# Query features of two groups in one set of products, and three calls of a hand-written schedule moved

## Chip, core and metric

The kernel runs on one core of a Trainium2 chip. The metric is the device time of one launch in microseconds (us). The median of three runs of the kernel before is 263.09 us (263.04 to 263.23). One more execution was taken with the hardware profiler: it took 262.89 us, and its trace spans 261.1 us. Clock times below ("at 62.89") are microseconds from the start of that trace.

The engines are TensorE (PE in the profile; its weight loads are PEld), VectorE (DVE), ScalarE (ACT), GpSimd (POOL) and SyncE (SP), which here only starts DMAs. Each works through its own list of instructions in order and waits on semaphores for the others.

## What is computed

An attention with polynomial features, followed by two dense layers with ELU between them. Batch, heads, rows and head size are 4, 4, 1088 and 32; `r` is 8; the dense layers are 128 to 2048 to 128.

```python
def phi(x):                                   # 64 features of a row
    a, b = x @ S1.T, x @ S2.T                 # 8 and 8
    return (a[..., :, None] * b[..., None, :]).reshape(..., 64)
q_p, k_p = phi(q), phi(k)
kv  = einsum('bhsf,bhsd->bhfd', k_p, v)       # per batch and head, 64 x 32
z   = k_p.sum(axis=2)                         # per batch and head, 64
num = einsum('bhsf,bhfd->bhsd', q_p, kv)
den = einsum('bhsf,bhf->bhs', q_p, z) + 1e-6
x   = (num / den), heads side by side         # 4352 rows of 128
h   = x @ w_in                                # 4352 x 2048
out = where(h > 0, h, exp(min(h, 0)) - 1) @ w_out
```

The denominator is computed without the 64 features: it is the sum over eight places of b times "b against z", and the program divides the factors by it (`an`) before it forms the 64 products.

## The kernel before

**Groups.** The 4352 rows make nine groups of 512 (the last has 256). Group `g` covers 16 tiles' worth of one batch: groups 2 and 3 are batch 1, tiles of 64 columns 0 to 7 and 8 to 15 of its transposed queries `qT[1]`.

**Steps.** The dense layers are done in 64 steps `(g, cp)`, where `cp` is one of eight pairs of 128 hidden columns. The list `steps` (L954) fixes their order: groups 0 and 1 alternate up to step 15, then groups 2, 3, ... follow with eight steps each. The loop at L1051 issues one step: `mm1` (first layer, PE, into two PSUM banks "h"), then whatever the schedule hangs on this step with `at`, then the ELU of the first half (`elu`: two ACT passes L811 and L813, one DVE pass L819 that writes `gg`), then the calls hung on with `mid`, the ELU of the second half, the calls of `late`, and last the second layer of the step before the previous one. That second layer is `mm2` or `mm2_blocks` for groups 0 and 1; from step 16 on it is `mm2_seven` (L720), which makes 7 block products out of 8 from sums that POOL forms: `sums7` (three POOL instructions per step, tile `tt`, L701 to L704) and `weights7` (L684, sums of the weights in `SS`, four POOL instructions per call).

**The attention is spread over these steps** by the table of `at`, `mid` and `late` calls (L970 to L1048). All engines are in order, so the place in this table is the place in each engine's queue. The parts that matter here:

- Keys of a batch: `transp` (DVE, 1088 columns) turns the keys; `KF_late` makes features on PE; `KO` the 64 products; `KA` (L425, PE) sums them against v; `sums_out` (L984) copies z on ACT (`ZC`), turns kv on DVE (`KT_out`, L436) and sends it through DRAM with five DMAs on SP; `turn` (`Z`, PE) and `turned` (`Z_out`, DVE, then `Z_share`, two POOL instructions) put z into the weights `SWs`.
- Queries of a group: `queries` (L658) takes the two "h" banks of the next step and two more banks, and issues into all four: the output products `q5` of one group (half f=0), the features `q1` (L533) of another, and `q5` again (f=1). `q1` is 16 products on 32x32 pieces of the array, one for each piece. `q1_out` (L544) is four DVE transposes out of the four banks into `abw`. Then on DVE come `q2_den` (L558: product, sum, reciprocal, product: the division), `q2_half` (L623, 64 products) and `q4` (L631, a transpose into `qpT`); `q5` and the ACT copies `q5_out` give the group's `xg`, the input of `mm1`. `q2_a` (L617) is an ACT copy of the divided factors into PSUM.

A "h" bank has four buffers, two per step, so the PE part of step n that writes the banks of step n+1 must wait for the DVE pass L819 of step n-1. The next `mm1` in turn must wait for the transposes that read them.

For batch 1 and the groups 2 and 3, the schedule before says:

```python
for b, (n_t, n_f, n_o, n_a, n_z) in enumerate(
        ((4, 6, (7, 9), 11, 12), (12, 16, (17, 18), 19, 20), (15, 16, (23, 24), 27, 28)), 1):
for n, g, nx in ((13, None, 2), (15, 2, 3), (22, 3, 4), (30, 4, 6), (46, 6, 8), (62, 8, None)):
    at(n, queries, g, nx, n + 1)
```

that is: sums of batch 1 in step 11, z in step 12, features of group 2 in step 13, output of group 2 with features of group 3 in step 15, output of group 3 with features of group 4 in step 22.

Of the kernel before, what the change touches and what calls it, by code (L numbers as in the profile page):

```python
# [12 lines left out]
F32 = mybir.dt.float32  # L13
# [9 lines left out]
def _ap(ap: bass.AP, free):  # L23
    return dataclasses.replace(ap, ap=[list(ap.ap[0])] + [list(x) for x in free])
# [3 lines left out]
def kernel(  # L28
# [21 lines left out]
    nc = tc.nc  # L50
    B, H, S, D = q.shape
    R = S1.shape[0]
    P = 128
# [3 lines left out]
    NP = NC // 2  # L57
# [7 lines left out]
    work = ctx.enter_context(tc.tile_pool(name="wk", bufs=2))  # L65
# [7 lines left out]
    qT = [const.tile([FD, NT, 64], F32, name=f"qT{b}") for b in range(2)] * 2  # L73
    qE = const.tile([FD, 2, 64], F32, name="qE")
# [69 lines left out]
    for x, (eng, src) in enumerate(((nc.sync, S1), (nc.scalar, S2))):  # L144
        rs = slice(R * x, R * x + R)
# [150 lines left out]
    SWs = const.tile([FD, B, 4, R], F32, name="SWs")  # L296
# [180 lines left out]
    NQ = (NH + 7) // 8  # L477
    qn = [min(8, NH - 8 * g) // 2 for g in range(NQ)]
    abw, ans, qp, qpT, xg, xps = {}, {}, {}, {}, {}, {}
# [48 lines left out]
    def quarter_of(g, w):  # L528

        n = un[g] // 2  # L530
        return (*half_tile(g + n * w // 8, n * w % 8), n)

    def q1(g, ps, o, opened):  # L533
        for w in range(4):
            b, t, n = quarter_of(g, w)
            qs = qE[:, b:b + 1, :] if g == NQ - 1 and b < 2 else qT[b][:, t:t + n, :]
            for r in range(4):
                rows = slice(32 * r, 32 * r + 32)
                nc.tensor.matmul(ps[r][32 * w:32 * w + 32, o:o + 64 * n], SWs[rows, b].rearrange("p x r -> p (x r)"),  # L539
                                 qs[rows].rearrange("p t s -> p (t s)"),  # L540
                                 start=not opened, stop=True, skip_group_check=True, tile_position=(32 * r, 32 * w))
        abw[g] = ps, o

    def q1_out(g):  # L544
        (ps, o), n = abw[g], un[g]
        pair = n > 4
        abw[g] = work.tile([P, H * n if pair else H * 4, 4 * R], F32, name="abw", tag="abwp" if pair else "abw",
                           bufs=1 if pair else 2)
        m = H * n // len(ps)
        for r in range(len(ps)):  # L550
            nc.vector.transpose(abw[g][:, m * r:m * r + m, :].rearrange("p m y -> p (m y)"),
                                ps[r][:, o:o + 32 * m])
# [105 lines left out]
    def queries(g5, g1, n):  # L658

        hs[steps[n]] = [psum.tile([P, 512], F32, name="h", tag="h", bufs=4) for c in range(2)]  # L660
        ps = hs[steps[n]] + [psum.tile([P, 512], F32, name="qps", tag="aux") for _ in range(2)]
        if g5 is not None:
            q5(g5, ps, 0)
        if g1 is not None:
            q1(g1, ps, 256 if g5 is not None else 0, g5 is not None)
        if g5 is not None:
            q5(g5, ps, 1)
# [293 lines left out]
    def at(n, f, *a):  # L961
        extra.setdefault(n, []).append((f, *a))

    def mid(n, f, *a):
        extra.setdefault((n, 0), []).append((f, *a))

    def late(n, f, *a):
        extra.setdefault((n, 1), []).append((f, *a))
# [25 lines left out]


    for b, (n_t, n_f, n_o, n_a, n_z) in enumerate(
            ((4, 6, (7, 9), 11, 12), (12, 16, (17, 18), 19, 20), (15, 16, (23, 24), 27, 28)), 1):
        (late if b == 2 else at)(n_t, transp, kT, "k", b, 0, NT)
        at(n_f, KF_late, b, n_f + 1 if b == 3 else None)
        (mid if b == 3 else late)(n_f, KF_late_out, b)  # L1000
        for half in range(2):
            if b == 1 and half == 0:
                at(n_o[half], KO, b, half, nc.gpsimd)
            else:
                late(n_o[half] - 1, KO_a, b, half)
                at(n_o[half], KO_b, b, half)
        at(n_a, KA, b)
        late(n_a, sums_out, b)
        at(n_z, turn, b)
        at(n_z, turned, b)  # L1010
# [1 line left out]
    at(19, transp, qT, "q", 2, 0, NT)  # L1012
    late(24, transp, qT, "q", 3, 0, NT)

    for n, g, nx in ((13, None, 2), (15, 2, 3), (22, 3, 4), (30, 4, 6), (46, 6, 8), (62, 8, None)):
        at(n, queries, g, nx, n + 1)
        if g is not None:
            mid(n, q5_out, g)
        if nx is not None:
            mid(n, q1_out, nx)  # L1020
        if g is not None and len(units[g]) > 1:
            late(n, q5_out, g, 1)
    late(13, q2_den, 2)
    late(13, q2_half, 2, 0)
    mid(14, q4, 2)
    late(19, q2_den, 3)
    late(19, q2_a, 3, 0)
    late(19, q2_half, 3, 0)
    late(20, q4, 3)
# [13 lines left out]
    late(59, q2_half, 8, 0)  # L1043
    late(60, q4, 8)

    late(12, weights7, slice(NP - 2, NP))
    late(13, weights7, slice(0, 3))
    late(15, weights7, slice(3, NP - 2))  # L1048

    N = len(steps)  # L1050
    for n in range(2, N):  # L1051
        g, cp = steps[n]
# [29 lines left out]
        g, cp = before  # L1082
# [10 lines left out]
    g = NQ - 2  # L1093
# [53 lines left out]
```

## Time and profile before

| | us |
|---|---|
| median of three runs | 263.09 |
| profiled execution | 262.89 |
| its span | 261.1 |
| PE busy in the span | 255.5 (98%) |
| DVE, ACT, POOL busy | 188.1, 183.2, 158.9 |
| step 14 (first layer, `mm2`, nothing else on PE) | 65.08 to 68.51 |
| step 18 (first layer, `mm2_seven`, nothing else on PE) | 81.26 to 84.50 |

The page of the profile gives the busy time of each engine, the chain of work that ended last, and groups of instructions. Its timeline lists each engine's instructions in order: start, time from the first start to the last end, line, operation, output and inputs, count, and in brackets how long the engine was idle before and what released it. One product of the program in fp32 can be recorded as two instructions, so the 16 products of `q1` appear as 32. The ends of matmuls are modelled; their starts are not, so lengths on PE are taken here from one start to the next. The granted PE clock is 9 tenths or more in all 40 slices of the span.

### The profile page before, as it was taken

What the parts mean: (1) busy time and instruction counts of PE and PEld (TensorE: products, weight loads), DVE (VectorE), ACT (ScalarE), POOL (GpSimd) and SP (SyncE); (2) the same over time, 40 slices, a digit from 0 to 9 for tenths busy, and PEclk for the clock granted to TensorE, in tenths of its full rate; (3) what the DMA queues carried; (4) which work ended last, traced back from release to release, by engine and by line L of the source; (5) the groups of instructions that cost most, each with busy time, mean ns of one, the idle gap of its engine ahead of it and who ended that gap; (6) DMA issues with size and microseconds to landing.
All of it is one profiled execution on the core that took longest, in us unless ns stands there. A gap on an engine that the chain in (4) does not pass through costs nothing.

```text
span 261.1 us, 9678 instructions
## 1 busy us (share of the span) xinstructions
PE 255.5 (98%) x4107; PEld 158.6 (61%) x4107; DVE 188.1 (72%) x356; ACT 183.2 (70%) x358; POOL 158.9 (61%) x202
## 2 busy tenths in 40 slices
PE   8899999999999999999999999999999999999994
PEld 7652333354346657666666666665666666668994
DVE  6899999999978987997477575744455446674641
ACT  2469878767568387775687777775877777777792
POOL 4420007006276978788678798888588888887410
PEclk9999999999999999999999999999999999999999
DMA  6998089022011111012100200020001100110021
GB/s 175 331 358 216 3 246 261 7 72 53 4 29 19 28 25 26 3 15 31 28 3 1 30 13 3 0 33 13 3 0 24 21 4 0 21 24 3 3 35 28
DMA packets 28506, 14.29 MB, mean 55 GB/s; under 512 B 21392, under 2 KB 26640, under 8 KB 28464
## 3 DMA queue, kind: packets, MB, share of 16 engines
q1 hardware_dynamic: 28032, 13.32, 20.7%
q8 instruction: 32, 0.52, 0.8%
q10 hardware_dynamic: 368, 0.30, 0.3%
q14 instruction: 10, 0.08, 0.1%
q0 software_dynamic: 64, 0.07, 0.1%
HBM read 11.31 MB, written 2.36 MB: 52 GB/s over the span
## 4 chain that ended last, share of the span: by engine, by line
PE 97%; DVE 1%; ACT 0%; issue 0%; DVEq 0%
PE h L256 45%; PE pb L740 17%; PE pa L740 13%; PE o L256 5%; PE pb L716 4%; PE ol L256 3%; PE idle L264 1%; PE h L645 1%; PE kv L430 1%; PE qps L645 1%; PE abp L340 1%; PE h L539 1%; PE qtp L598 1%; DVE qp L586 1%; PE xps L605 0%; PE kfps L362 0%
## 5 line engine op out<-in xcount | busy, mean ns | idle before, releaser
L256 PE MATMUL h<-xg,W 128*32 128x512 f32 (+3 forms) x880 | 130.6, 538 | 0.4 <-ACT xg L611 0.4
L819 DVE SCALAR_TENSOR_TENSOR gg<-e,h 128x512 f32<-128x512 f32 x128 | 85.7, 681 | 51.7 <-ACT e L813 48.3
L811 ACT ACTIVATE e<-h 128x512 f32<-128x512 f32 x128 | 75.5, 590 | 42.9 <-PE h L256 42.8
L813 ACT ACTIVATE e<-e 128x512 f32<-128x512 f32 x128 | 80.9, 632 | 3.8
L701 POOL TENSOR_TENSOR tt<-gg 128x512 f32<-128x512 f32 x50 | 64.2, 1285 | 30.0 <-DVE gg L819 24.9
L256 PEld LDWEIGHTS h<-xg,W 128*32 128x32 f32 (+1 forms) x880 | 42.5, 123 | 43.3 <-issue 34.9
L704 POOL TENSOR_TENSOR tt<-gg,tt 128x256 f32<-128x256 f32 x50 | 36.9, 738 | 3.9
L703 POOL TENSOR_TENSOR tt<-tt,gg 128x256 f32<-128x256 f32 x50 | 36.8, 735 | 3.9
L740 PEld LDWEIGHTS pa<-gg,W 128*64 128x64 f32 (+1 forms) x472 | 23.8, 128 | 24.0 <-issue 23.3
L740 PE MATMUL pa<-gg,W 128*64 128x128 f32 (+1 forms) x472 | 30.4, 274 | 0.0
L740 PE MATMUL pb<-tt,SS 128*64 128x128 f32 (+1 forms) x456 | 29.4, 273 | 0.0
L740 PEld LDWEIGHTS pb<-tt,SS 128*64 128x64 f32 (+1 forms) x456 | 22.6, 128 | 0.0
L740 PE MATMUL pa<-tt,SS 128*64 128x128 f32 (+1 forms) x276 | 20.9, 273 | 0.0
L740 PE MATMUL pb<-tt,W 128*64 128x128 f32 (+1 forms) x244 | 19.7, 273 | 0.0
L740 PE MATMUL pb<-gg,SS 128*64 128x128 f32 (+1 forms) x244 | 19.7, 273 | 0.0
L134 POOL TENSOR_TENSOR raw<-raw,tiny 128x512 f32<-128x512 f32 x1 | 1.0, 1044 | 24.7 <-DVE raw L129 24.7
L256 PE MATMUL o<-gg,W 128*32 128x512 f32 x128 | 15.3, 595 | 0.0
L740 PEld LDWEIGHTS pa<-tt,SS 128*64 128x64 f32 (+1 forms) x276 | 13.5, 125 | 0.0
L740 PEld LDWEIGHTS pb<-gg,SS 128*64 128x64 f32 (+1 forms) x244 | 12.6, 127 | 0.0
L740 PEld LDWEIGHTS pb<-tt,W 128*64 128x64 f32 (+1 forms) x244 | 12.6, 127 | 0.0
L716 PE MATMUL pb<-gg,W 128*32 128x256 f32 x192 | 11.6, 380 | 0.0
L871 DVE SCALAR_TENSOR_TENSOR gg<-e,h 128x256 f32<-128x256 f32 x16 | 6.6, 418 | 6.4 <-PE h L256 3.2
(156 smaller groups left out, 274.3 us busy)
## 6 DMA issues: line engine op xcount, KB each, us to landing
raw<-in_moe_w_in_dram SPq DMA_DIRECT2D x8, 256.0 KB, 6.2
raw<-in_moe_w_out_dram SPq DMA_DIRECT2D x8, 256.0 KB, 6.5
out_dram<-ob SPq DMA_DIRECT2D x112, 16.0 KB, 1.6
hd_k<-in_k_dram SPq DMA_DIRECT2D x3, 544.0 KB, 7.8
hd_q<-in_q_dram SPq DMA_DIRECT2D x3, 544.0 KB, 8.1
v<-in_v_dram SPq DMA_DIRECT2D x4, 288.0 KB, 7.0
v<-in_v_dram SPq DMA_DIRECT2D x4, 256.0 KB, 8.5
kvs<-kvd SPq DMA_DIRECT2D x13, 32.0 KB, 1.8
```

The costliest lines, as they stand in the source:

```text
L256: nc.tensor.matmul(dst[c:c + tile], lhs[:, c:c + tile], rhs, skip_group_check=True, tile_position=(0, c), **kw)
L264: nc.tensor.matmul(idle[c:c + tile, :cols], ones[:, :tile], ones[:, :cols], skip_group_check=True, tile_position=(0, c))
L645: nc.tensor.matmul(ps[w][32 * r:32 * r + 32, :64 * n], kvs[b][rows, r, f, :], qpT[g, i][rows, o:o + 2 * n, f, :], start=(f == 0), stop=(f ...
L701: nc.gpsimd.tensor_tensor(_ap(t[:, 0], [[4 * P, 2], [P, 2], [1, P]]), _ap(gs[g, cp][:, 0, P:], [[4 * P, 2]] + us), _ap(gs[g, cp][:, 0], [[ ...
L703: nc.gpsimd.tensor_tensor(t[:, 1], t[:, 2], b11, op=ADD)
L704: nc.gpsimd.tensor_tensor(t[:, 3], b21, t[:, 1], op=SUB)
L716: nc.tensor.matmul(acc[1][0][r:r + width[0], 256 * hi:256 * hi + 256], lhs[:, w:w + width[0]], gg[:, c, 256 * u:256 * u + 256], start=(cp ...
L740: nc.tensor.matmul(bank[r:r + width[0], P * col:P * col + P], lhs[:, w:w + width[0]], rhs[:, u], start=(first and i in ((0,) if g == 1 els ...
L811: nc.scalar.activation(e, hs[g, cp][c][:, :n], RELU, scale=-1.0)
L813: nc.scalar.activation(e, e, EXP, scale=-1.0)
L819: nc.vector.scalar_tensor_tensor(gs[g, cp][:, c, :n], es[g, cp][:, c, :n], -1.0, hs[g, cp][c][:, :n], op0=ADD, op1=MAX)
L871: nc.vector.scalar_tensor_tensor(gs["last", k // 2][:, k % 2, :2 * P], es["last", k // 2][:, k % 2, :2 * P], -1.0, hs["last", k][:, :2 * P ...
```

## The change

`q1` of group 2 now takes the same 128 columns of group 3 along: each of its 16 products streams 256 columns in two pieces, tile t and tile t+8. It is issued in step 12 instead of 13, and `q1` of group 3 is gone from step 15. Two of its four transposes come ahead of the ELU of step 12, two in the middle of it, each for both groups, into one tile `abw2`. To have z in time, batch 1's `KA` and `sums_out` go from step 11 to 10, `turn` and `turned` from 12 to 11. The turning of batch 2's keys goes from step 12 to 14. `q2_den` of group 2 goes from late in step 13 to late in step 12, its `q4` from the middle of step 14 to its beginning, and `q2_den` of group 3 from late in step 19 to the middle of step 15. Of POOL's `weights7`, the last two pairs stay in step 12 but earlier, pairs 0 to 2 go from step 13 to 15 and pairs 3 to 5 from 15 to 16.

```diff
     def q1(g, ps, o, opened):
         for w in range(4):
             b, t, n = quarter_of(g, w)
-            qs = qE[:, b:b + 1, :] if g == NQ - 1 and b < 2 else qT[b][:, t:t + n, :]
+            m, qs = 64 * n, qE[:, b:b + 1, :] if g == NQ - 1 and b < 2 else qT[b][:, t:t + n, :]
+            qs = qs.rearrange("p t s -> p (t s)")
+            if g == 2:
+                m, qs = 2 * m, _ap(qs, [[8 * 64, 2], [1, m]])
             for r in range(4):
                 rows = slice(32 * r, 32 * r + 32)
-                nc.tensor.matmul(ps[r][32 * w:32 * w + 32, o:o + 64 * n], SWs[rows, b].rearrange("p x r -> p (x r)"),
-                                 qs[rows].rearrange("p t s -> p (t s)"),
-                                 start=not opened, stop=True, skip_group_check=True, tile_position=(32 * r, 32 * w))
+                nc.tensor.matmul(ps[r][32 * w:32 * w + 32, o:o + m], SWs[rows, b].rearrange("p x r -> p (x r)"),
+                                 qs[rows], start=not opened, stop=True, skip_group_check=True,
+                                 tile_position=(32 * r, 32 * w))
         abw[g] = ps, o
+
+    def q1_out_two(rs):
+        if 3 not in abw:
+            abw[2, 3] = abw[2][0]
+            t = work.tile([P, 2, 4 * H, 4 * R], F32, name="abw2", tag="abw2", bufs=1)
+            abw[2], abw[3] = t[:, 0], t[:, 1]
+            abw[2, 0] = t
+        n = 4 * H // 4
+        for r in rs:
+            nc.vector.transpose(abw[2, 0][:, :, n * r:n * r + n, :].rearrange("p g m y -> p g (m y)"),
+                                abw[2, 3][r][:, :64 * n].rearrange("p (g m) -> p g m", g=2))
...
-            ((4, 6, (7, 9), 11, 12), (12, 16, (17, 18), 19, 20), (15, 16, (23, 24), 27, 28)), 1):
+            ((4, 6, (7, 9), 10, 11), (14, 16, (17, 18), 19, 20), (15, 16, (23, 24), 27, 28)), 1):
...
-    for n, g, nx in ((13, None, 2), (15, 2, 3), (22, 3, 4), (30, 4, 6), (46, 6, 8), (62, 8, None)):
+    for n, g, nx in ((12, None, 2), (15, 2, None), (22, 3, 4), (30, 4, 6), (46, 6, 8), (62, 8, None)):
         at(n, queries, g, nx, n + 1)
         if g is not None:
             mid(n, q5_out, g)
-        if nx is not None:
+        if nx == 2:
+            at(n, weights7, slice(NP - 2, NP))
+            at(n, q1_out_two, (0, 1))
+            mid(n, q1_out_two, (2, 3))
+        elif nx is not None:
             mid(n, q1_out, nx)
...
-    late(13, q2_den, 2)
+    late(12, q2_den, 2)
     late(13, q2_half, 2, 0)
-    mid(14, q4, 2)
-    late(19, q2_den, 3)
+    at(14, q4, 2)
+    mid(15, q2_den, 3)
     late(19, q2_a, 3, 0)
...
-    late(12, weights7, slice(NP - 2, NP))
-    late(13, weights7, slice(0, 3))
-    late(15, weights7, slice(3, NP - 2))
+    late(15, weights7, slice(0, 3))
+    late(16, weights7, slice(3, NP - 2))
```

## Prediction

> **What bounds the kernel now.** I read the busy times and the chain of waits on the page first.
>
> ```profile
> PE 255.5 (98%) x4107; PEld 158.6 (61%) x4107; DVE 188.1 (72%) x356; ACT 183.2 (70%) x358; POOL 158.9 (61%) x202
> ...
> PE 97%; DVE 1%; ACT 0%; issue 0%; DVEq 0%
> ```
>
> PE is both the busiest engine and 97% of the chain that ends last. So time is won only where PE gets less work, or where it loses time that its busy count hides. The waits of PE, for the whole span, name five, all in the start-up (2.0 us together); asked from 50 us on, the view is empty. But ends on PE are modelled, so a wait can hide inside a "busy" stretch. I therefore took PE's timeline and compared steps from start to start. A bare step with `mm2` is 3.43 (step 14, 65.08 to 68.51), one with `mm2_seven` 3.24 (step 18). What a step has over that is the price of its extras:
>
> ```profile
> 61.02 1.94 PE L256 MATMUL h<-xg,W 128*32 128x512 f32 x16
> 62.89 0.30 PE L539 MATMUL h<-qT,SWs 32*32 32x128 f32 x2
> ...
> 63.33 1.94 PE L716 MATMUL pb<-gg,W 128*32 128x256 f32 x32
> 65.08 1.91 PE L256 MATMUL h<-xg,W 128*32 128x512 f32 x16
> ...
> 68.51 1.91 PE L256 MATMUL h<-xg,W 128*32 128x512 f32 x16
> 70.35 0.30 PE L645 MATMUL h<-qpT,kvs 32*32 32x128 f32 x2
> ...
> 70.67 0.41 PE L539 MATMUL h<-qT,SWs 32*32 32x128 f32 x3
> ...
> 71.16 0.31 PE L645 MATMUL h<-qpT,kvs 32*32 32x128 f32 x2
> ...
> 71.76 1.93 PE L256 MATMUL o<-gg,W 128*32 128x512 f32 x16
> 73.50 1.90 PE L256 MATMUL h<-xg,W 128*32 128x512 f32 x16
> ```
>
> Step 13 takes 65.08 - 61.02 = 4.06, so `q1` of group 2 costs 4.06 - 3.43 = 0.63. Step 15 takes 73.50 - 68.51 = 4.99: its three stages (`q5`, `q1` of group 3, `q5`) cost 1.56, the middle one 71.16 - 70.67 = 0.49 of it.
>
> Step 22 has the same three stages, with 256 columns in `q1`:
>
> ```profile
> 95.47 1.94 PE L256 MATMUL h<-xg,W 128*32 128x512 f32 x16
> 97.34 0.67 PE L645 MATMUL h<-qpT,kvs 32*32 32x128 f32 x3
> 97.72 0.30 PE L645 MATMUL qps<-qpT,kvs 32*32 32x128 f32 x2
> ...
> 100.88 0.61 PE L256 MATMUL h<-xg,W 128*32 128x512 f32 x4
> ```
>
> It takes 5.41, 2.17 over 3.24. Per piece of the array, steps 15, 46 and 30 stream 384, 576 and 768 columns in such three stages, and cost 1.56, 1.88 (179.20 to 184.33) and 2.22 (125.07 to 130.53): a line of 0.66 / 384 = 1.72 ns a column. Step 22 with 512 should cost 1.78. It costs 0.39 more, and the gap from 97.34 to 97.72 is where: the second bank is not free. DVE, ACT and POOL tell why.
>
> ```profile
> 92.01 0.27 ACT L621 COPY qa<-an 128x128 f32<-128x128 f32 x1 [3.91 <-DVE an L573]
> ```
> ```profile
> 90.55 1.28 POOL L701 TENSOR_TENSOR tt<-gg 128x512 f32<-128x512 f32 x1
> ```
> ```profile
> 90.59 1.39 DVE L573 TENSOR_TENSOR an<-abw,den 128x128 f32<-128x128 f32 x1
> ...
> 96.41 1.25 DVE L819 SCALAR_TENSOR_TENSOR gg<-e,h 128x512 f32<-128x512 f32 x2
> ```
>
> `q2_den` of group 3, late in step 19, ends at 91.98. ACT's copy of `an` stands in front of the ELU of step 20, so ACT idles 3.91 us, and starts on a bank that PE finished some 2 us earlier. ACT works without a gap until 98.06 to catch up; the `gg` of step 21 end at 97.66, and at 97.72 PE goes on. L573 itself takes 1.39, where the same line took 0.29 at 66.39 with POOL idle; here it ends 0.15 after POOL's L701.
>
> **Part by part.**
>
> *One `q1` of 256 columns.* Removed: 0.63 (step 13), and the middle stage of step 15. What step 15 keeps is bounded twice: 1.56 - 0.49 = 1.07, and step 62, which has `q5` twice with 64 columns each and no `q1` (233.01 to 237.19, 4.18 - 3.24 = 0.94), plus 128 columns more, 0.22, = 1.16. I take 1.10, nearer to the same step's own row. Added in step 12: 0.63 + 128 x 1.72 ns = 0.85 (bounds: 0.10 more than now, the difference of the rows of 0.30 and 0.40 for one product of 128 and 256, and 0.63 more, two separate stages). Sum: 2.19 now, 1.95 then: **-0.24**; with the ends of 1.07 to 1.16 and 0.73 to 0.85, -0.18 to -0.39; with the outermost 1.26 even +0.2. That the columns come in two pieces should not matter: `q5` reads its columns in pieces too and lies on the same line.
>
> [...]
>
> *`KA` and `Z` one step earlier.* The same products, 1.18 and 0.07, in another step: 0 for PE if nothing is late. `KA` would start at 49.48 + 1.72 = 51.2; the last of its inputs, L389, ends at 50.10. ACT's copy of z follows its ELU of step 10 (ended at 53.0); `Z` comes on PE at 55.9. The kv transpose (0.24) now stands ahead of the turning of `qT[1]` (1.31), which ends near 56.4, and z comes behind it at 56.9 (it waits for `Z`, done by 56.2; behind it stand the `gg` of step 11); POOL's two (0.42) make `SWs` ready by 57.4. SP's DMAs of batch 1 are now issued earlier, though behind the same held load of the last queries, whose buffer frees with `qT[1]`, 0.2 later; before, the last was issued by 64.4 and such a one lands in 1.8; `q5` wants them at 70.5.
>
> *Step 12.* Steps 11, 12, 13 start on PE at 54.09, 57.59 and 61.87. `q1` starts near 59.4 and needs the `gg` of step 11, done near 58.3: 1.1 to spare. The tightest place is behind it: `mm1` of step 13 needs the first two transposes. DVE first rounds the last weights (57.86 to 60.37 now, 2.51; now waiting for ACT until 58.3), to 60.8. They wait for `q1` itself too, but it is through by 60.3; a later one would hold all of DVE's queue, the `gg` of step 12 first. A pair of 256-column transposes takes 0.78 (99.68), so they are read out at 61.2 and 61.6. Margin 0.6, and 1.1 for the second bank. Cost 0; each us beyond costs one.
>
> *Group 2 to step 15.* The division of group 2 ends at 64.7 (1.26 as now, POOL's sums over at 62.6), `gg` of step 13 at 66.0, products (1.15) and turn (1.17) at 68.3, `gg` of step 14 at 69.5; `q5` starts at 70.5. Margin 1.0, against 0.1 now (70.27 to 70.35). DVE is then behind by the two key turns (2.45, one of them new here) and the division of group 3 (1.26): the second `gg` of step 15 ends at 74.4, as it does now (74.48), and the output turn at 75.1. PE writes that bank at 76.3. No cost.
>
> *`weights7`.* 4 x 0.6 = 2.35 on POOL goes from idle time (62.87, step 13) to behind the sums of step 15 in place of the other block, which follows the sums of step 16. POOL's sums of step 17 so begin at 85.0 instead of 84.78 and end at 87.9. PE's `mm2_seven` of step 19 needs the last of them at its seventh product, 88.5: 0.6 to spare.
>
> *Division of group 3 off step 19.* DVE loses 2.5 there (89.50 to 91.98), ACT copies at 88.2, the `gg` of step 21 end near 96.2, and PE wants the bank at 97.1. **The hidden 0.39 goes.** Next late are those `gg` themselves, with 0.9 to spare. In its new place POOL is free but for a 0.23 copy, because POOL's next sums wait for the `gg` that stands behind the division.
>
> [...]
>
> After step 22 every step is 3.24 or 3.25 with no hidden gap, to the end, so what is won stays won.
>
> Sum: -0.24 - 0.39 = **-0.63**: 262.89 to 262.26 for a profiled execution. The median lies 0.20 above that execution, so 262.5.
>
> **Rivals.**
>
> 1. *Only the products count* (14%). The gap in step 22 stays, because ACT or POOL is late there for another reason: -0.24, 262.85. For it: ACT is nearly full from 92 to 98. Against: its 3.91 idle names `an`.
>
> 2. *PE waits for the transposes in step 13* (10%). If rounding or transposes end over 0.6 late, the excess is paid; a us late leaves -0.23, 262.85. Against: the four rounding rows are even (0.43 to 0.72).
>
> [...]
>
> 4. *The long product does not run as one.* If 256 columns in two pieces cost two stages, +0.2 instead of -0.24, with the gap gone -0.2: 262.9. Counted with the forecast's spread.
>
> **Chances.** Forecast 70%: its spread of -0.2 to -0.8 us (the ends of the first part with 0.39) is faster by over 0.2% (0.53 us, about what a measurement here can tell from no change) in 57 of the 70, within it in 13. Rival 1, 14, within. Rival 2: 8 within, 2 slower. Rival 3: 6 slower. Together 57, 35, 8. The range 262.2 to 263.1 takes in the forecast's ends, 262.3 to 262.9, with 0.1 for the spread of the runs (263.04 to 263.23), and rivals 1, 2 and 4; rival 3 lies outside.
>
> **What will show it.** Step 12 on PE about 0.85 over 3.43 and step 15 about 1.10 over; step 22 about 1.78 over 3.24, with no gap in its first `q5`; ACT's `qa` copy without its idle. Wrong if a step from 12 to 21 is longer than 3.43 or 3.24 plus its extras: in 13 through L551's successor, in 19 through `tt`.

## The result, and the profile after

The changed kernel takes 262.60 us (median of 19 runs, 262.30 to 263.15), the kernel before 263.08 (19 runs): a ratio of 0.9983, 95% interval 0.9976 to 0.9991. That is 0.48 us less; the forecast, 262.5, would have been 0.58 less than this median. Over three series (42 runs) the changed kernel's median is 262.62.

The first profiled execution after took 263.07 us, with a span of 261.1, as before. It is one of the long ones of its series, whose median span is 260.6. What made it long can be seen, and is taken up below. The page gives the same picture of the bound, with 32 matmul records fewer on PE (16 products in two records each):

```profile
PE 255.4 (98%) x4075; PEld 158.9 (61%) x4075; DVE 186.6 (71%) x352; ACT 183.3 (70%) x358; POOL 158.9 (61%) x202
...
PE 97%; DVE 1%; ACT 0%; issue 0%; DVEq 0%
```

Lines of the changed kernel from L557 on have numbers that are 14 higher (L649 is L635 of before), and `q1`'s product is now L542. PE's timeline of step 12, from the start of its first layer to that of step 13:

```profile
57.58 1.94 PE L256 MATMUL h<-xg,W 128*32 128x512 f32 x16
59.45 0.41 PE L542 MATMUL h<-qT,SWs 32*32 32x256 f32 x2
...
60.10 1.93 PE L256 MATMUL o<-gg,W 128*32 128x512 f32 x16
61.84 0.62 PE L256 MATMUL h<-xg,W 128*32 128x512 f32 x4
```

The step is 61.84 - 57.58 = 4.26 long, 0.83 over a bare 3.43. Step 15 has the two stages of `q5` left:

```profile
68.72 1.91 PE L256 MATMUL h<-xg,W 128*32 128x512 f32 x16
70.56 0.30 PE L659 MATMUL h<-qpT,kvs 32*32 32x128 f32 x2
...
71.55 1.93 PE L256 MATMUL o<-gg,W 128*32 128x512 f32 x16
73.30 1.04 PE L256 MATMUL h<-xg,W 128*32 128x512 f32 x8
```

It is 4.58 long, 1.15 over. ACT no longer idles before its copy of group 3's divided factors; the division that it waited for is now done on DVE 14 us ahead of the copy, and L587 takes 0.29 there, where the same product (L573) took 1.39 before. First ACT, then DVE:

```profile
87.97 0.28 ACT L635 COPY qa<-an 128x128 f32<-128x128 f32 x1
```
```profile
72.59 0.28 DVE L577 TENSOR_TENSOR pw<-abw 128x128 f32<-128x128 f32 x1
...
73.54 0.29 DVE L587 TENSOR_TENSOR an<-abw,den 128x128 f32<-128x128 f32 x1
```

Step 22, here from a second profile of the same kernel (e1 below, span 260.6), no longer has the gap inside its first `q5`:

```profile
95.42 1.94 PE L256 MATMUL h<-xg,W 128*32 128x512 f32 x16
97.29 0.30 PE L659 MATMUL h<-qpT,kvs 32*32 32x128 f32 x2
...
100.47 1.04 PE L256 MATMUL h<-xg,W 128*32 128x512 f32 x8
```

It takes 5.05 instead of 5.41 (5.14 in the first profile).

**What made the first profile long** is in step 19, in the middle of the short products of `KA`. In the timeline of PE and of its weight loads, "issue" after the arrow means that the engine waited for nothing that the profile shows:

```profile
86.58 0.28 PE L430 MATMUL kv<-kp,v 128*32 128x64 f32 x4
87.03 0.24 PE L430 MATMUL kv<-kp,v 128*32 128x64 f32 x1 [0.17 <-issue]
```
```profile
87.02 0.11 PEld L430 LDWEIGHTS kv<-kp,v 128*32 128x32 f32 x1 [0.33 <-issue]
```

PE stood still for some 0.4 us, and step 19 took 4.83 instead of 4.41.

### The profile page after: what moved, and what is told of

Its sections match the earlier page's. It is cut to its first block, busy times and chain, and to the rows that moved or that the text cites. A ratio compares the mean times of both kernels' runs of the same rounds, so it can differ in the third digit from the quotient of the medians.

```text
span 261.1 us, 9610 instructions
## 1 busy us (share of the span) xinstructions
PE 255.4 (98%) x4075; PEld 158.9 (61%) x4075; DVE 186.6 (71%) x352; ACT 183.3 (70%) x358; POOL 158.9 (61%) x202
## 4 chain that ended last, share of the span: by engine, by line
PE 97%; DVE 1%; ACT 0%; issue 0%; DVEq 0%
PE h L256 45%; PE pb L754 17%; PE pa L754 13%; PE o L256 5%; PE pb L730 4%; PE ol L256 3%; PE kv L430 1%; PE idle L264 1%; PE h L659 1%; PE abp L340 1%; PE qps L659 1%; PE h L542 1%; PE qtp L612 1%; DVE qp L600 0%; PE xps L619 0%; PE kfps L362 0%
## 5 line engine op out<-in xcount | busy, mean ns | idle before, releaser
L256 PEld LDWEIGHTS h<-xg,W 128*32 128x32 f32 (+1 forms) x880 | 43.2, 123 | 42.6 <-issue 34.0
```

Of the source, the lines that this page charges most:

```text
L256: nc.tensor.matmul(dst[c:c + tile], lhs[:, c:c + tile], rhs, skip_group_check=True, tile_position=(0, c), **kw)
```

## The experiments

Length of each step on PE in the profiled execution, from start to start of the first layer (us), and the sum of steps 10 to 22:

| kernel | 10 | 11 | 12 | 13 | 15 | 18 | 19 | 22 | 10 to 22 |
|---|---|---|---|---|---|---|---|---|---|
| before | 3.43 | 4.61 | 3.50 | 4.06 | 4.99 | 3.24 | 4.41 | 5.41 | 51.40 |
| changed, first profile | 4.60 | 3.51 | 4.26 | 3.44 | 4.58 | 3.25 | 4.83 | 5.14 | 51.34 |
| changed, again (e1) | 4.59 | 3.51 | 4.26 | 3.44 | 4.57 | 3.24 | 4.41 | 5.05 | 50.83 |
| changed, third (e10) | 4.59 | 3.51 | 4.27 | 3.44 | 4.58 | 3.24 | 4.86 | 5.07 | 51.31 |
| division back (e2) | 4.60 | 3.51 | 4.26 | 3.44 | 4.58 | 3.25 | 4.41 | 5.60 | 51.38 |
| division alone (e3) | 3.43 | 4.60 | 3.50 | 4.06 | 4.99 | 3.25 | 4.41 | 5.05 | 51.04 |
| joined in step 13 (e4) | 3.43 | 4.60 | 3.50 | 4.27 | 4.86 | 3.24 | 4.41 | 5.39 | 51.45 |
| weight sums back (e5) | 4.59 | 3.51 | 4.27 | 3.44 | 4.58 | 3.25 | 4.41 | 5.05 | 50.83 |
| division, sums early (e6) | 4.60 | 3.51 | 3.49 | 4.04 | 5.00 | 3.24 | 4.41 | 5.05 | 51.08 |
| transposes late (e7) | 4.60 | 3.51 | 5.02 | 3.47 | 4.57 | 3.25 | 4.41 | 5.05 | 51.61 |
| weight sums together (e8) | 4.59 | 3.51 | 4.27 | 3.44 | 4.58 | 4.26 | 4.41 | 5.05 | 51.84 |
| division alone again (e9) | 3.43 | 4.60 | 3.50 | 4.06 | 4.99 | 3.25 | 4.41 | 5.05 | 51.04 |
| division, sums early again (e11) | 4.59 | 3.51 | 3.47 | 4.04 | 5.00 | 3.25 | 4.41 | 5.05 | 51.06 |
| sums early, z not (e12) | 4.59 | 3.44 | 3.53 | 4.04 | 5.08 | 3.25 | 4.41 | 5.05 | 51.13 |

Times of the same kernels, with the ratio to the kernel before on the same chip. "Outside" is the time less the span, a mean over the runs:

| kernel | time, median | ratio, 95% interval | span, median | outside |
|---|---|---|---|---|
| before (beside e1 to e4) | 263.05 | | 261.2 | 1.85 |
| e1, changed again | 262.60 | 0.9981 (0.9970 to 0.9992) | 260.6 | 1.96 |
| e2, division back | 263.27 | 1.0001 (0.9991 to 1.0011) | 261.2 | 1.98 |
| e3, division alone | 262.62 | 0.9976 (0.9967 to 0.9986) | 260.75 | 1.86 |
| e4, joined in step 13 | 263.14 | 1.0001 (0.9990 to 1.0012) | 261.3 | 1.87 |
| before (beside e5 to e8) | 263.10 | | 261.3 | 1.84 |
| e5, weight sums back | 262.58 | 0.9977 (0.9966 to 0.9988) | 260.6 | 1.94 |
| e6, division, sums early | 262.96 | 0.9993 (0.9985 to 1.0002) | 260.9 | 1.97 |
| e7, transposes late | 263.49 | 1.0018 (1.0007 to 1.0029) | 261.4 | 2.01 |
| e8, weight sums together | 263.84 | 1.0027 (1.0017 to 1.0038) | 261.8 | 1.99 |
| before (beside e9 to e12) | 263.12 | | 261.3 | 1.86 |
| e9, division alone again | 262.71 | 0.9987 (0.9978 to 0.9996) | 260.9 | 1.83 |
| e10, changed, third | 262.76 | 0.9987 (0.9978 to 0.9996) | 260.7 | 2.01 |
| e11, division, sums early again | 263.08 | 1.0001 (0.9986 to 1.0016) | 261.15 | 1.98 |
| e12, sums early, z not | 263.04 | 0.9993 (0.9984 to 1.0002) | 261.0 | 1.97 |

### The changed kernel again (e1, e10)

No edit.

> The changed kernel, nothing altered. Theory: the 0.43 us in which PE had no instruction in step 19 of the first profiled execution (263.07 us, where the median of 19 was 262.6) belongs to that execution, not to the program: this one should span about 260.6, with step 19 at 4.4 as before the change, step 12 at 4.26, step 15 at 4.58 and step 22 between 5.0 and 5.15; ratio 0.998. Rival: the gap belongs to the program; then it is there again at the same place and the span is 261.1.

The second profile has no gap in step 19 and a span of 260.6; the third has it again (4.86, span 261.2). So it is neither a single accident nor there in each execution, and both theories as stated miss. What goes with it is the queue that the page names "q8 instruction" (32 transfers, 0.52 MB). Seven profiles are of kernels with the joined products and the early sums (first, e1, e2, e5, e7, e8, e10). In all of them one such transfer starts between 1.8 before and 0.0 before the start of step 19. In the two with the gap it lands 1.40 and 1.51 us after that start (it took 1.47 and 1.53); in the other five it lands at 0.98 or earlier. In e4, which joins the products but leaves the sums in step 11, it starts 0.8 before the step and lands at 0.62: no gap either. In the kernel before, and in e3, e6, e9, e11 and e12, whose products are not joined, the transfer near this place starts some 1.5 after step 19 has begun, and none of them has the gap. So the place of the transfer goes with the joined products. That PE waited for it is not shown: the trace doesn't name the transfer as what PE waited for, and no run moved the transfer alone.

### Division back, division alone (e2, e3, e9)

```diff
 e2, to the changed kernel:        e3 and e9, to the kernel before:
-    mid(15, q2_den, 3)            -    late(19, q2_den, 3)
+    late(19, q2_den, 3)           +    mid(15, q2_den, 3)
```

> The changed kernel, but group 3's division late in step 19 again. Theory (two separate gains): the joined products stay, worth 0.2; the wait in step 22 is back, and step 22 takes about 5.4 instead of 5.0 to 5.15; ACT's copy of the divided factors again idles 3 to 4 us; the time is some 0.3 above the changed kernel, 262.85. Rival: the gain is the joined products alone, and the time equals the changed kernel's 262.6.

> The kernel before, with group 3's division alone moved to the middle of step 15, behind group 3's transposes. Theory: step 22 loses its wait and goes from 5.41 to 5.0 to 5.15, ratio 0.999 (262.75 to 262.8); steps 13 and 15 on PE stay at 4.06 and 4.99. VectorE's output turn of step 15 comes at 75.6 instead of 74.4, still ahead of PE's 76.5. Rival: the division needs the earlier transposes of the joined products; here it makes the second half of step 15's ELU late and PE waits in step 16 or 17, time 263.1 or more.

With the division back in step 19 the whole gain is gone, 1.0001, although PE keeps its 0.2 of the joined products up to step 21. ACT's and PE's timelines of e2:

```profile
91.91 0.27 ACT L635 COPY qa<-an 128x128 f32<-128x128 f32 x1 [4.09 <-DVE an L587]
```
```profile
97.05 0.40 PE L659 MATMUL h<-qpT,kvs 32*32 32x128 f32 x2
97.61 0.29 PE L659 MATMUL h<-qpT,kvs 32*32 32x128 f32 x1 [0.16 <-DVE gg L833]
```

PE comes to `q5` at 97.05, 0.29 earlier than before, and goes on at 97.61, 0.11 earlier: the wait is 0.56 instead of 0.38, and the step 5.60 instead of 5.41. Now even the waits name DVE's `gg`. Where the 0.2 was lost can be followed back. Up to step 19 DVE had come along with PE: its `gg` of step 18 begin 0.29 earlier. It loses the lead in the division. DVE, the kernel before and then e2:

```profile
88.17 1.25 DVE L819 SCALAR_TENSOR_TENSOR gg<-e,h 128x512 f32<-128x512 f32 x2
89.50 0.43 DVE L563 TENSOR_TENSOR pw<-abw 128x128 f32<-128x128 f32 x1
```
```profile
87.88 1.26 DVE L833 SCALAR_TENSOR_TENSOR gg<-e,h 128x512 f32<-128x512 f32 x2
89.21 0.63 DVE L577 TENSOR_TENSOR pw<-abw 128x128 f32<-128x128 f32 x1
90.50 1.38 DVE L587 TENSOR_TENSOR an<-abw,den 128x128 f32<-128x128 f32 x1
```

In both kernels the two products of the division end 0.15 or 0.16 after an instruction of POOL, not a fixed time after their own start: `an` ended at 91.98 behind POOL's 91.83 in the kernel before, and at 91.88 behind POOL's 91.72 in e2. So the division ran by POOL's clock here, and POOL had come only 0.1 earlier. POOL, the kernel before and then e2:

```profile
84.78 1.28 POOL L701 TENSOR_TENSOR tt<-gg 128x512 f32<-128x512 f32 x1 [2.11 <-DVE gg L819]
```
```profile
84.16 0.60 POOL L702 TENSOR_TENSOR SS<-W,SS 128x192 f32<-128x192 f32 x1
84.72 1.29 POOL L715 TENSOR_TENSOR tt<-gg 128x512 f32<-128x512 f32 x1
90.45 1.27 POOL L715 TENSOR_TENSOR tt<-gg 128x512 f32<-128x512 f32 x1
```

Before the change POOL waited for `gg` there, which ended at 84.70. In e2 that `gg` ended at 84.42, but POOL was still at the moved weight sums. e5, which differs from e1 by these sums alone and whose steps start within 0.02 of e1's there, begins the same instruction at 84.72 where e1 begins it at 85.12. So a part of the change that costs PE nothing by itself kept POOL, and with it the division, ACT's copy and the `gg` of step 21, within 0.1 of where they had been. The division back together with the weight sums back was not run, so it is not shown whether the joined products would keep their 0.2 there. Both theories fail for e2: the gain that stays alone isn't the products', and in this arrangement the two gains don't add.

The division alone gives 0.9976, as much as the whole change, and step 22 takes 5.05. The output turn of step 15 (L839) comes at 74.97, 0.6 sooner than expected, and ahead of PE's product at 76.6. The repetition:

> The same kernel as the division alone, again, on one chip with the next three. Theory (joined products take 0.2 off PE, but the early sums that they need cost 0.1 outside the span): time 262.62 and span 260.75 again, level with the changed kernel. Rival: the earlier figure was of that chip and hour; then it lies 0.15 or more above the changed kernel.

It lay at 262.71, the changed kernel beside it (e10) at 262.76, with the same ratio and interval.

> The changed kernel again, beside the division alone and the early sums. Theory: span 260.6, time outside the span 1.97, time 262.6. Rival: beside the others on one chip it is 0.15 or more faster than the division alone, as its steps on PE say (50.83 against 51.04 for steps 10 to 22).

So the 0.21 by which PE's steps are shorter in the changed kernel (50.83 against 51.04) is not seen in the time. It is in the spans, 260.6 against 260.75 and 260.7 against 260.9; outside the span the changed kernel takes 0.1 and 0.18 more.

### Joined products in step 13 (e4)

```diff
 to the kernel before, with the new q1 and q1_out_two:
-    for n, g, nx in ((13, None, 2), (15, 2, 3), (22, 3, 4), ...
+    for n, g, nx in ((13, None, 2), (15, 2, None), (22, 3, 4), ...
...
+        if nx == 2:
+            mid(n, q1_out_two, (0, 1, 2, 3))
```

> The kernel before, with the joined products of 256 columns alone: in step 13, all four transposes in the middle of that step; sums of batch 1 in step 11 and the division in step 19 as before. Theory: PE saves 0.2 in steps 13 and 15 together, but the longer transposes (1.45 instead of 0.84) make everything behind them on VectorE 0.6 later, and the output products of group 2 in step 15, which had 0.1 to spare, wait some 0.35 for the second half of step 14's ELU: time 263.1 to 263.3, ratio 1.000. Rival: step 12 was not needed, and the time is 262.85.

Step 13 becomes 0.21 longer and step 15 0.13 shorter instead of 0.41: its first `q5` waits for `gg` of step 14. In the trace of e4 the start to start of its first two rows is 0.30, where it was 0.01 in the changed kernel (70.56 and 70.57):

```profile
70.98 0.59 PE L659 MATMUL h<-qpT,kvs 32*32 32x128 f32 x3
71.28 0.30 PE L659 MATMUL qps<-qpT,kvs 32*32 32x128 f32 x2
```

DVE's second `gg` of step 14 ended at 71.22 there. Time 1.0001, as the theory said. Step 12 is needed to keep the 0.2 on PE.

### Weight sums back, and together (e5, e8)

```diff
 e5: the three calls of weights7 as in the kernel before (late 12, 13, 15)
 e8:
-    late(16, weights7, slice(3, NP - 2))
+    late(15, weights7, slice(3, NP - 2))
```

> The changed kernel with GpSimd's three blocks of weight sums where they were before (late in steps 12, 13 and 15). Theory: they cost PE nothing in either place, so every step on PE stays within 0.02 of the changed kernel's and the span stays 260.6; if the 0.12 that the changed kernel has outside its span (time less span 1.98, against 1.86 before) hangs on this move, the time is 262.45 to 262.5, else 262.6. Rival: GpSimd's place matters; then steps 17 to 19 on PE differ by 0.1 or more.

> The changed kernel with both large blocks of weight sums late in step 15, so that GpSimd's sums for step 16's products start 2.35 later. Theory: GpSimd has 0.6 to 1.0 to spare here, so PE waits some 1.0 in step 18 (third product of seven), once, and the span is 261.6. Rival: GpSimd's queue has more room than read, and the span stays 260.6.

e5 is the changed kernel to 0.02 in every step: with the division moved, the move of the weight sums does nothing to PE, and the time outside the span doesn't hang on it. In e8, POOL starts the sums of step 16 at 82.03, and PE waits where the expectation said, for the middle one of the three (PE first, then POOL):

```profile
84.18 0.42 PE L754 MATMUL pa<-tt,SS 128*32 128x128 f32 x8 [0.80 <-POOL tt L717]
```
```profile
82.03 1.29 POOL L715 TENSOR_TENSOR tt<-gg 128x512 f32<-128x512 f32 x1
83.40 0.73 POOL L717 TENSOR_TENSOR tt<-tt,gg 128x256 f32<-128x256 f32 x1
```

Step 18 is 1.01 longer and the later ones unchanged; POOL has caught up by step 19. The time rose by 1.26 over e5 in the same series, 0.25 more than the step shows.

### Transposes late (e7)

```diff
-            at(n, q1_out_two, (0, 1))
-            mid(n, q1_out_two, (2, 3))
+            late(n, q1_out_two, (0, 1, 2, 3))
```

> The changed kernel with all four transposes behind both halves of step 12's ELU. Theory: the first two are read out 0.7 to 1.0 later than PE wants them, where the changed kernel had some 0.6 to spare; PE waits about 0.6 at the start of step 13's first layer, nothing else is late, and the span grows by about 0.6 to 261.2, if the later wait in step 22 doesn't come back. Rival: the margin is wider than read from the trace and nothing changes, 260.6.

The first transpose starts at 62.66, 1.1 after the end of the rounding; PE's next first layer waits:

```profile
63.16 1.92 PE L256 MATMUL h<-xg,W 128*32 128x512 f32 x16 [0.56 <-DVE abw L555]
```

Step 12 is 5.02 instead of 4.26. Over steps 10 to 22 PE loses 0.78, more than the 0.6 expected; the time is 0.91 above e5's. Step 22's wait stays away.

### Early sums without the joined products (e6, e11, e12)

```diff
 e6 and e11, to the division alone:                      e12: ... (7, 9), 10, 12)
-            ((4, 6, (7, 9), 11, 12), (12, 16, ...
+            ((4, 6, (7, 9), 10, 11), (12, 16, ...
```

> The kernel before with the division of group 3 in step 15 and batch 1's sums and z one step earlier, and nothing joined. Theory: moving the sums costs PE nothing (4.60 and 3.50 move from steps 11 and 12 to 10 and 11), so the span is that of the division alone, 260.75, and the time 262.6. Rival: the earlier sums are what costs the changed kernel 0.12 outside the span, or some wait in step 10 or 11; then 262.75.

> The division and the early sums and z of batch 1, nothing joined, again. Theory: the early sums cost 0.1 outside the span (1.97 against 1.86) and 0.1 to 0.2 within it that no step from 10 on shows: time 262.9. Rival: the 262.96 of the first time was chance, and it lies at 262.62 to 262.75.

> The division, and batch 1's sums one step earlier with z left in step 12; nothing joined. It tells which of the two moves carries the time outside the span: if the sums on PE and their DMAs, 1.97; if z alone, 1.86. PE's steps 10 to 22 add up to 51.04 in any case.

Moving the sums costs PE 0.04 in steps 10 to 22 of e6, as good as nothing, and yet e6 lies 0.34 above e3, the division alone, and above both times that were expected. 0.11 of it is outside the span. The median span is 0.15 longer than e3's, but no longer than that of the repetition e9 (260.9), so a cost inside the span isn't shown; and e3 was measured in another series, beside a kernel before that was 0.05 faster. e11's runs spread from 262.62 to 265.20, and its profile was disturbed in the start-up (span 263.3), so it decides little; its 1.98 outside the span agrees. In e12, z stays in step 12 and the 1.97 is there all the same, so it goes with the sums and not with z; PE loses 0.09 in e12, mostly in step 15 (5.08). Against e9, on the same chip, e12 lies 0.33 higher by the medians, 0.14 of it outside the span.

e6 also tells what the joined products are worth in the time. e5, in the same series, has them and the calls moved with them on top of e6: 262.58 against 262.96, with a span of 260.6 against 260.9 and 50.83 against 51.08 in steps 10 to 22. The intervals of the two ratios still overlap a little.

Over all series the time outside the span is 1.83 to 1.87 in the kernels that have batch 1's sums in step 11 (before, e3, e4, e9), and 1.94 to 2.01 in the runs that have them in step 10 (nine in the table, and the first series with 2.00). Why sums in the middle of the program lengthen what lies outside its span, no run here tells.

## Why the prediction was right, and where it was not

*Range, sign and place held.* 262.60 lies 0.1 above the 262.5, and the forecast's two terms are in the trace where they had been put. The prediction gave 57 chances in 100 to a gain of over 0.2%; at 0.17% it fell to the 35 that were given to a change within 0.2%. Its sign of being wrong, a step from 12 to 21 longer than its extras, showed in step 19 of two of three profiles, though not through POOL's `tt`.

*The joined products, -0.24.* Measured on PE: 0.83 added in step 12 (0.85 forecast), 1.15 left in step 15 (1.10 taken, 1.16 the upper bound), so steps 10 to 15 together are 0.20 shorter (24.02 before, 23.82 after). The price per column, read from three other steps, served well; of the two bounds for step 15 the one from another step was right, not the nearer row.

*The hidden wait, -0.39.* Step 22 went from 5.41 to 5.05, -0.36, and e3 shows that the division alone does it. The chain named in the prediction (DVE's division, ACT's copy, the ELU behind it, the bank) is the one that e2 brings back with all its links. Its first link is POOL: behind POOL's sums the division took 2.48 (89.50 to 91.98), in its new place 1.24 (72.59 to 73.83). The difference is three times the wait of 0.38, so, as an estimate, a division in step 19 that didn't wait for POOL would have left no gap either.

*Moved at no cost to PE.* Transposes, turned keys, weight sums and z cost PE nothing, as worked out; e7 and e8 show that the two margins were real, by using them up. One reading missed without effect: SP's DMAs of batch 1 were not issued earlier, the last four from 63.14 to 64.89 in the first profile, from 61.96 to 64.37 before; `q5` began at 70.56. POOL did not delay the division in its new place: DVE began L577 at 72.59 and it took 0.28, L587 0.29. POOL's copy (L485) began at 72.61 and took 0.37, where it had taken 0.23 before.

*What failed, first: the price of the joined products by themselves.* Rival 1 gave them alone -0.24 and 262.85. e2, which has the products without the division's move, has the 0.20 in steps 10 to 15, and nothing at the end: 1.0001. The moved weight sums had been priced only against PE's `mm2_seven` of step 19. In e2 they hold POOL, `an` ends 0.16 after POOL's instruction, and the wait in step 22 grows from 0.38 to 0.56, by what PE had gained before it.

*Second: that the total reaches the time.* With the division moved, the terms do add on PE: 51.40 to 50.83 in steps 10 to 22 (e1), -0.57 where -0.63 had been worked out, and the median span fell by 0.6 (261.2 to 260.6). The time fell by 0.48. The sums of batch 1, put at 0 for their move to an earlier step, cost PE next to nothing, but with them came 0.12 outside the span (1.85 to about 1.97), where the prediction had no term; and two of the three profiled executions have the gap of 0.4 in step 19. The joined products show in the time against e6, which has the early sums too (0.38 by the medians, 0.25 in PE's steps), and not beyond the noise against the division alone (262.60 and 262.62, 262.76 and 262.71): what they win, the early sums that they need cost again. The division was worth the whole gain by itself (0.9976). "What is won stays won" was thus true of PE's steps 23 and on and not of the time. That the forecast nevertheless came within 0.1 is partly luck: nothing in it bounded the cost outside the span, which happened to be small.

*Rival 2's price* (each us of late transposes costs one) holds to size in the steps: 0.78 in e7, though the time rose by 0.91. Of *rival 3*, the 6 chances in 100 that POOL makes the kernel slower, no run shows the cause: in the middle of step 15 the two products of the division took 0.28 and 0.29, and 0.35 and 0.29 in e3. What PE pays when POOL is late, e8 shows: 1.01 in step 18, and 1.26 in the time.

## What to carry to other kernels

A step that is longer than its neighbours by start-to-start times shows a wait that the busy share and the list of waits hide; here it was worth more (0.36 us in step 22) than the products that the change saves (0.20). Before adding two gains, ask whether one lies ahead of a wait for another engine, and by whose clock that engine runs there: in e2 PE's 0.2 was lost again, because POOL, further up the chain, had been given work that kept it from coming along. A move that costs nothing in one arrangement has to be priced again in the next. And look for the copy that stands in front of an engine's regular work: moving the four small instructions that it waited for, out of the stage where they took 2.48 us beside POOL's sums, to one where they took 1.24 (1.30 in e3), gave all of the measured gain.

## What was not expected of the hardware

In two of three profiles of the changed kernel, PE stood still for 0.4 us in a burst of 64-column products, waiting for nothing that the profile shows, and in both a 16 KB transfer of the instruction queue that begins with this step had taken 1.47 and 1.53 us; in the six other profiles with the joined products it did not, and the transfer had landed by 0.98 us after the start of the step. With 16 products fewer ahead of it, the transfer near this place started 1.8 to 0.0 us before step 19, where it had started some 1.5 us after the step had begun. The time outside the profiled span differs between kernels that do the same work by 0.1 us (1.83 to 1.87 against 1.94 to 2.01), which a span alone doesn't show. And the two 128x128 products of the division on VectorE took 0.27 to 0.29 us with POOL idle (from 65.45 before, from 63.43 after), and 0.43 and 1.39 (before) or 0.63 and 1.38 (e2) beside POOL's sums in step 19, ending 0.15 or 0.16 after one of them.
